# Three fused blocks on one core: engines in source order, weight preparation in equal portions at fixed places, the value product two steps later, VectorE a step behind ScalarE, five weight tiles in flight

## The chip, the core and the metric

The kernel runs on one core of a Trainium2 chip. The core has five engines with queues of their own, each of which runs its queue in order: TensorE (PE in the profile, its weight loads PEld), VectorE (DVE), ScalarE (ACT), GpSimd (POOL) and SyncE (SP), which only issues DMAs. Sixteen DMA engines move data between main memory (HBM) and the on-chip memory SBUF; matmuls write to the eight banks of PSUM. The metric is device time in microseconds.

## The reference

Attention with capped scores on (4 batches, 12 heads, 448 tokens, 64 dims), then two pairs of matmuls (two layers) on 1792 x 768, with inner width 2048. All in float32.

```python
scores = cap * np.tanh(q @ k.T / np.sqrt(64) / cap)
attn = softmax(scores)                        # over the keys
x = (attn @ v)                                # heads side by side: 1792 x 768
h = np.maximum(x @ w_in, 0.0);  y = h * h @ w_out
h = y @ w2_in;  out = h / (1 + exp(-1.702 * h)) @ w2_out
```

## The kernel before

One function, `bounded_cap`, does the whole work (a second one, `any_cap`, is for caps over 40 and is skipped by a branch at the end).

**Attention** goes over 24 pairs of heads. Time is counted in steps T of the source; pair n starts at T = 8n, and `PLAN` (lines 877 to 890) says which function runs how many steps after the start: `load_pair` at -17, key and query transposes and splits (`prep_k`, `prep_q`) from -8 to -3, and for each of four key chunks c the scores product on TensorE (`scores`, L832) at 2c, tanh on ScalarE (L842) at 2c+1, exp on ScalarE (L846) at 2c+2 and the product with v (`pv`, L858) at 2c+3. `take_x` (copies of the two value banks, on ScalarE and VectorE) comes at 10, `divide` (reciprocal on VectorE, multiply on GpSimd, L874, and the store of x) at 11. Within a step the oldest pair comes first. A float32 product in the layers and in the scores is done as three products of a high and a low part (hi x hi, hi x lo, lo x hi); the high part is a rounding copy on ScalarE, the low part a subtraction on VectorE.

**Weight preparation.** The layers multiply 2 x 2 blocks by the seven-product scheme of Strassen and Winograd, so each weight block is turned once into seven matrices that are stored in HBM (`wsa`, `wsb`). One chunk of this is `chunk_steps` (L901): two `load`s of raw weights (64-bit words, of which the wanted bits are joined), two `join`s (L934 on ScalarE, L936 on VectorE), and `sums` (L957 to L960) of four operations, on GpSimd during attention and on VectorE later, with four stores (L947). There are 34 chunks. `weight_group` puts some in a list, `weight_work` pops them in the proportion of the steps gone: 7 chunks over T = 10 to 112, 4 over 130 to 196, then 5 or 6 in each first-product stage (`A_WORK`) and 1 + 2 in a second-product stage (`B_WORK`).

**Layers.** Each of two layers is done in two halves (pairs of batches). In the first-product stage ("a", 56 products of 9 matmuls) a product needs one weight tile of 192 KB, in the second ("b", 21 products of 24 matmuls) two of 256 KB. `load_grain` brings a tile into `wf` (3 buffers) by SyncE's queue, `split_grain` makes the high part (L1047) and the low part (L1048), four tiles ahead of their product (`W_AHEAD`). `split_form` (L1079, L1080) does the same for the moving operands, `x_step` loads and combines those of a half, by SyncE's queue, `b_step` those of the second product from the results of the first. `product` (L1071) issues the matmuls, `after` what reads their banks, `result` the stores, of the last layer alternately by SyncE's and ScalarE's queues.

**What sets the order.** The kernel is written in a language whose scheduler builds each engine's queue: the source gives priorities, and the scheduler moves instructions ahead where it finds their inputs ready in its own model of time. So the place of an instruction in the source is not its place in the queue; the DMA issues of SyncE and GpSimd are moved in the same way. Buffers of a pool are handed out in rotation, and who takes one waits for its last reader.

Of the kernel before, what the change touches and what calls it, by code (L numbers as in the profile page):

```python
# [677 lines left out]
def bounded_cap(ctx, tc, q, k, v, cap, w1, w2, w3, w4, out):  # L678
# [6 lines left out]
    P = 128  # L685
# [18 lines left out]
    w_p = ctx.enter_context(tc.tile_pool(name="w", bufs=6))  # L704
    wf_p = ctx.enter_context(tc.tile_pool(name="wf", bufs=3))
# [7 lines left out]
    e_p = att.enter_context(tc.tile_pool(name="e", bufs=4, side="right"))  # L713
    x_p = att.enter_context(tc.tile_pool(name="x", bufs=3, side="right"))
    ps_m = att.enter_context(tc.tile_pool(name="ps_m", bufs=3, space=PSUM))
    ps_s = att.enter_context(tc.tile_pool(name="ps_s", bufs=2, space=PSUM))
    ps_x = att.enter_context(tc.tile_pool(name="ps_x", bufs=1, space=PSUM))

# [4 lines left out]
    a_ = nc.scalar  # L723

# [146 lines left out]
    def divide(b, p):  # L871
        x, ct = x32.pop((b, p)), pvp.pop((b, p))[2]
        v_.reciprocal(ct, ct)  # L873
        nc.gpsimd.tensor_tensor(x, x, ct, ALU.mult)  # L874
        Q_PUT.dma_start(out=xs[b, p], in_=x)
# [4 lines left out]
        -7: [(prep_k, 1)],  # L880
        -6: [(prep_k, 2), (load_v,)],
        -5: [(prep_q, 0)],
        -4: [(prep_q, 1)],
        -3: [(prep_q, 2)],
# [16 lines left out]
    def chunk_steps(l, kind, i):  # L901
# [25 lines left out]
        def join(u):  # L927
            t = st.pop(("r", u))[:, : 2 * n]

            def words(dt):  # L930
                return t.bitcast(dt).rearrange("p k (f e) -> p k f e", f=P)

            z = sx.bitcast(F16)[:, : 2 * n].rearrange("p k (f t) -> p k f t", t=2)[:, :, :, 1]
            a_.activation(z, words(BF16)[:, :, :, 2], AF.Copy)  # L934
            y = st[u] = y_p.tile([P, 6, P], F32, tag="y", name="wy")
            v_.scalar_tensor_tensor(  # L936
                y[:, : 2 * n].bitcast(I32), words(I32)[:, :, :, 0], 13, sx[:, : 2 * n],
                ALU.logical_shift_right, ALU.bitwise_or,
            )
# [9 lines left out]
        def sums():  # L949
            y1, y2 = st[0], st[1]  # L950
            s = y_p.tile([P, 6, P], F32, tag="y", name="ws")
            t = y_p.tile([P, 3, P], F32, tag="yt", name="wt", bufs=1)
            a11, a12, a21, a22 = (y[:, h * n : h * n + n] for y in (y1, y2) for h in range(2))
            s1, s2 = (s[:, h * n : h * n + n] for h in range(2))
            put(0, y1, 2)
            e = eng[0]
# [10 lines left out]
    eng = [nc.gpsimd]  # L967
# [8 lines left out]
    def weight_group(m):  # L976

        now = [todo.pop(0) for _ in range(m)]
        for n, (load, join, sums) in enumerate(now):
            nxt = now[n + 1][0] if n + 1 < m else lambda u: None  # L980
            if n == 0:
                work.extend([(load, 0), (load, 1)])
            work.extend([(join, 0), (nxt, 0), (join, 1), (sums,), (nxt, 1)])

    def weight_work(k, m):

        if k == 0:
            work_all[0] = len(work)
        while work_all[0] - len(work) < (k + 1) * work_all[0] // m:
            f, *a = work.pop(0)  # L990
            f(*a)

    work_all = [0]
# [44 lines left out]
    def split_grain(n):  # L1038
# [9 lines left out]
        v_.tensor_tensor(y, src, f32(x), ALU.subtract)  # L1048
# [28 lines left out]
    def split_form(key, src, n):  # L1077
        f = forms[key] = f_p.tile([P, 2, NX, S], F32R, tag="f", name="form")
        a_.activation(f[:, 0, :n, :], src, AF.Copy)  # L1079
        v_.tensor_tensor(f[:, 1, :n, :], src, f32(f[:, 0, :n, :]), ALU.subtract)  # L1080

    xin = {}

# [4 lines left out]
    def x_step(l, c, step):  # L1088
# [11 lines left out]
        def sub(o, x, y):  # L1100
            v_.tensor_tensor(xin[o], xin[x], xin[y], ALU.subtract)  # L1101

        if step == 0:
            get("t", left, 0)
            get("u", right, 0)
            form(1, "t")
        elif step == 1:
            get("w", right, NX)
            sub("t", "u", "t")
            form(5, "t")  # L1110
        elif step == 2:
            sub("t", "w", "t")
            form(6, "t")
        elif step == 3:
            sub("u", "w", "u")
            form(7, "u")
            get("u", left, NX)
        elif step == 4:
            form(2, "u")
        elif step == 5:  # L1120
            sub("t", "u", "t")
            form(4, "t")
        else:
            form(3, "w")

    def b_step(l, c, s, ch):
# [4 lines left out]
        def sub(o, x, y):  # L1131
            v_.tensor_tensor(o, x, y, ALU.subtract)  # L1132
# [9 lines left out]
        elif s == 6:  # L1142
            t = gt["t", ch] = wide("tl")[:, :n]
            sub(t, g22, g11)
            form(t)
        elif s == 7:
            sub(g12, g22, g12)
# [25 lines left out]
    def result(l, c, row, col, d, y):  # L1173
# [4 lines left out]
        o = small("t", 2).rearrange("p (c d) -> p c d", d=32)  # L1178
# [57 lines left out]
    if True:  # L1236
        T = -17
        emit_const()
        END = 8 * (len(pairs) - 1) + max(PLAN)
        while T <= END:  # L1240
            attn_sub(T)
            for (t0, t1), m in ATT_WORK:
                if T == t0:
                    weight_group(m)
                if t0 <= T < t1:
                    weight_work(T - t0, t1 - t0)
            if T in X_AT:
                x_step(0, 0, X_AT.index(T))
            if T in G_AT:
                n = G_AT.index(T)  # L1250
                load_grain(n)
                if n:
                    split_grain(n - 1)
            T += 1
        eng[0] = v_
        att.close()
        pool["g"] = ctx.enter_context(tc.tile_pool(name="g", bufs=1, side="right"))
        pool["q"] = ctx.enter_context(tc.tile_pool(name="q", bufs=3, side="right"))
        pool["pa"] = ctx.enter_context(tc.tile_pool(name="pa", bufs=5, space=PSUM))
        pool["pb"] = ctx.enter_context(tc.tile_pool(name="pb", bufs=3, space=PSUM))  # L1260
        loaded, split = len(G_AT), len(G_AT) - 1
        for u, (l, c, kind, s, i) in enumerate(seq):
            if (kind, s, i) == ("a", 1, 0):
                new_g()
                place = {"a": 0, "b": 0}
                if u == 0:
                    hi, lo = wt[0]
                    for n in range(3):
                        b = pool["pb"].tile([P, 512], F32, tag="b", name="pb")
                        nc.tensor.matmul(b[:, :S], hi[:, 0, :], forms[0, 0, "a", 1, 0][:, 0, 0, :], start=True, stop=True)  # L1270
            product(u)
            after(u)
            while split < min(gpos[u] + W_AHEAD + 1, len(grains)):
                if loaded <= split:
                    load_grain(loaded)
                    loaded += 1
                split_grain(split)
                split += 1
                load_grain(loaded)
                loaded += 1  # L1280
            nxt = (l, c + 1) if c == 0 else (l + 1, 0)
            if kind == "a":
                k, order = place["a"], (5, 6, 2)
                if i == NJ - 1 and s in order:
                    b_step(l, c, 1, order.index(s))
                if k == 0:
                    weight_group(A_WORK.get((l, c), 0))
                if k < 7 * NJ - 2:
                    weight_work(k, 7 * NJ - 2)
            else:  # L1290
                k, order = place["b"], (1, 2, 6, 7, 4, 5, 3)
                for (t0, t1), m in B_WORK.get((l, c), ()):
                    if k == t0:
                        weight_group(m)
                    if t0 <= k < t1:
                        weight_work(k - t0, t1 - t0)
                n = order.index(s) + 1
                if n < 7:
                    b_step(l, c, order[n], i)
                if nxt[0] < 2:  # L1300
                    if s == 5 and i == 2:
                        x_step(*nxt, 0)
                    elif s == 3:
                        for st in ((1, 2), (3,), (4, 5, 6))[i]:
                            x_step(*nxt, st)
            place[kind] += 1
# [59 lines left out]
```

## Time and profile before

| | us |
|---|---|
| runs | 1240.38, 1234.47, 1240.67 (median 1240.38) |
| profiled execution, its own time | 1234.58 |
| its span | 1232.7 |
| TensorE busy (matmuls) | 1103.8 (90%) |
| VectorE busy | 845.7 (69%) |
| ScalarE busy | 733.8 (60%) |
| GpSimd busy | 273.8 (22%) |
| mean granted TensorE clock | 0.97 of full speed |

The busy times are sums over the whole span; stages differ much, so the rows below are read by stretches. Matmuls overlap, and a busy TensorE is not one at its peak: the count of matmuls in a stretch says more. In a row of waits the engine and line that waited stand first, then what it waited for.

### The profile page before, as it was taken

To read this page: it belongs to the slowest core of one execution; us is meant where nothing else is said; L and a number is where in the kernel's file an instruction comes from. 1 tells how busy PE (TensorE), PEld (TensorE's weight loads), DVE (VectorE), ACT (ScalarE), POOL (GpSimd) and SP (SyncE) were. 2 spreads that over 40 slices of the span, in tenths; PEclk is the share of its full clock that TensorE was granted. 3 is DMA by queue.
4 is the path that set the end of the run, shared out by engine and by line. 5 is a ranking of instruction groups with operands and counts; after the bars stand their busy time and mean duration, and the time that the engine had idled before them with its cause. 6 is when DMAs were issued, how large, how long until landed. Compare 5 with 4: busy or idle time off the path is not lost.

```text
span 1232.7 us, 15718 instructions
## 1 busy us (share of the span) xinstructions
PE 1103.8 (90%) x5115; PEld 904.7 (73%) x5115; DVE 845.7 (69%) x1089; ACT 733.8 (60%) x1121; POOL 273.8 (22%) x367
## 2 busy tenths in 40 slices
PE   6588988769799999978799999878999998999997
PEld 3244444434489999877679999767999987999996
DVE  3656567858755598585566976677699676559953
ACT  4568777868755666544456655455575536556640
POOL 4657111776510002113310021243000000000000
PEclk9898999989999999998899999989999999999999
DMA  8988434989663338658863576688436464333544
GB/s 213 287 238 261 104 97 118 291 254 299 224 204 108 110 119 275 207 159 299 290 232 114 159 247 192 222 292 259 142 118 189 136 125 131 110 107 123 126 126 73
DMA packets 203757, 227.55 MB, mean 185 GB/s; under 512 B 123794, under 2 KB 160338, under 8 KB 203666
## 3 DMA queue, kind: packets, MB, share of 16 engines
q1 hardware_dynamic: 153234, 118.40, 34.3%
q0 software_dynamic: 28160, 105.30, 25.6%
q10 hardware_dynamic: 22272, 2.76, 1.6%
q8 instruction: 42, 0.69, 0.2%
q14 instruction: 49, 0.40, 0.1%
HBM read 165.84 MB, written 60.56 MB: 184 GB/s over the span
## 4 chain that ended last, share of the span: by engine, by line
PE 46%; DMA 12%; DVE 7%; issue 4%; ACT 3%; POOL 1%; SPq 0%; DVEq 0%; ACTq 0%; POOLq 0%
PE pa L1071 26%; PE pb L1071 20%; DMA wf<-wsa 7%; DMA wf<-wsb 3%; DVE wl L1048 2%; DVE form L1080 2%; ACT form L1079 1%; ACT sx L934 1%; ACT wh L1047 1%; DVE wy L936 1%; DMA wsa<-wy 1%; DVE qu L1201 0%; DVE xl L1101 0%; DMA xl<-ys 0%; DMA wsb<-wy 0%
## 5 line engine op out<-in xcount | busy, mean ns | idle before, releaser
L1071 PE MATMUL pa<-form,wh 128*128 128x448 f32 x1536 | 440.5, 368 | 5.3 <-DVE x L869 2.3
L1047 ACT ACTIVATE wh<-wf 128x384 fp32r<-128x384 f32 (+1 forms) x392 | 219.0, 566 | 306.5 <-DMA wf<-wsa 126.8
L1071 PE MATMUL pb<-form,wh 128*128 128x448 f32 x1152 | 338.5, 376 | 42.0 <-ACT qu L1198 21.7
L1048 DVE TENSOR_TENSOR wl<-wf,wh 128x384 fp32r<-128x384 f32 (+1 forms) x392 | 239.9, 620 | 136.0 <-ACT wh L1047 59.0
L1071 PEld LDWEIGHTS pa<-form,wh 128*128 128x128 f32 x1536 | 290.2, 189 | 32.0 <-DVE x L869 2.7
L1071 PE MATMUL pa<-form,wl 128*128 128x448 f32 x768 | 281.9, 367 | 0.1
L1071 PEld LDWEIGHTS pb<-form,wh 128*128 128x128 f32 x1152 | 219.3, 192 | 70.4 <-ACT qu L1198 28.0
L1071 PE MATMUL pb<-form,wl 128*128 128x448 f32 x576 | 215.4, 374 | 0.7 <-DVE wl L1048 0.7
L858 PE MATMUL vps<-e,v 128*128 128x448 f32 (+1 forms) x384 | 161.9, 594 | 57.1 <-ACT e L846 53.1
L1071 PEld LDWEIGHTS pa<-form,wl 128*128 128x128 f32 x768 | 144.8, 189 | 13.2 <-DVE wl L1048 0.4
L858 PEld LDWEIGHTS vps<-e,v 128*128 128x128 f32 (+1 forms) x384 | 61.4, 198 | 111.9 <-ACT e L846 70.8
L1071 PEld LDWEIGHTS pb<-form,wl 128*128 128x128 f32 x576 | 110.7, 192 | 11.7 <-DVE wl L1048 1.6
L1080 DVE TENSOR_TENSOR form<-g,form 128x1344 fp32r<-128x1344 f32 (+1 forms) x72 | 100.1, 1398 | 18.5 <-ACT form L1079 18.3
L936 DVE SCALAR_TENSOR_TENSOR wy<-wraw,sx 128x768 int32<-128x768 int32 (+1 forms) x68 | 68.0, 1000 | 63.4 <-ACT sx L934 37.3
L832 PE MATMUL sps<-qq,kk 64*128 64x448 f32 (+1 forms) x504 | 103.6, 452 | 5.4 <-ACT e L842 3.0
L934 ACT ACTIVATE sx<-wraw 128x768 f16<-128x768 bf16 (+1 forms) x68 | 69.4, 1020 | 51.9 <-DMA wraw<-in_moe_w_out_dram 20.7
L842 ACT ACTIVATE e<-sps 128x896 f32<-128x896 f32 x96 | 77.6, 812 | 30.6 <-PE sps L832 30.3
L1079 ACT ACTIVATE form<-g 128x1344 fp32r<-128x1344 f32 (+1 forms) x72 | 85.6, 1194 | 10.6 <-DVE g L1132 5.6
L832 PEld LDWEIGHTS sps<-qq,kk 64*128 64x128 f32 (+1 forms) x504 | 55.1, 198 | 49.2 <-issue 24.8
L846 ACT ACTIVATE e<-e,ecap 128x896 f32<-128x896 f32 x96 | 90.2, 944 | 1.8
L873 DVE RECIPROCAL ct<-ct 128x448 f32<-128x448 f32 x24 | 70.8, 2952 | 0.5
L1201 DVE SCALAR_TENSOR_TENSOR g<-pa,qu 128x448 f32<-128x448 f32 x64 | 39.9, 623 | 31.5 <-PE pa L1071 17.2
(76 smaller groups left out, 954.7 us busy)
## 6 DMA issues: line engine op xcount, KB each, us to landing
wf<-wsa SPq DMA_DIRECT2D x224, 192.0 KB, 2.5
wf<-wsb SPq DMA_DIRECT2D x168, 256.0 KB, 2.8
wraw<-in_moe_w_in_dram POOLq DMA_DIRECT2D x32, 766.5 KB, 8.1
wraw<-in_moe_w_out_dram POOLq DMA_DIRECT2D x48, 383.2 KB, 6.4
wsa<-wy POOLq DMA_DIRECT2D x32, 384.0 KB, 6.3
wsb<-wy POOLq DMA_DIRECT2D x24, 384.0 KB, 5.1
wsa<-ws POOLq DMA_DIRECT2D x16, 384.0 KB, 4.8
wraw<-in_moe_w_out_dram POOLq DMA_DIRECT2D x24, 255.5 KB, 5.7
```

The lines of the kernel that those rows point to most:

```text
L832: nc.tensor.matmul(ps[:, u, :S], x, y, start=all(t[0] != u for t in todo[:n]), stop=all(t[0] != u for t in todo[n + 1 :]),)
L842: a_.activation(e, chunk(c, sc.pop((b, p, c)))[:, :, :S], AF.Tanh)
L846: a_.activation(e, e, AF.Exp, scale=ecap)
L858: nc.tensor.matmul(pvp[b, p][j][:, :S], x.rearrange("p a d -> p (a d)"), t, start=c == 0, stop=c == TAIL,)
L873: v_.reciprocal(ct, ct)
L934: a_.activation(z, words(BF16)[:, :, :, 2], AF.Copy)
L936: v_.scalar_tensor_tensor(y[:, : 2 * n].bitcast(I32), words(I32)[:, :, :, 0], 13, sx[:, : 2 * n], ALU.logical_shift_right, ALU.bitwise_or,)
L1047: a_.activation(x, src, AF.Copy)
L1048: v_.tensor_tensor(y, src, f32(x), ALU.subtract)
L1071: nc.tensor.matmul(ps[:, :S], a[:, kk % 4, :], r, start=(s in (1, 5) and kk == 0 and n == 0), stop=(kk == ks - 1 and n == 2), skip_group_c ...
L1079: a_.activation(f[:, 0, :n, :], src, AF.Copy)
L1080: v_.tensor_tensor(f[:, 1, :n, :], src, f32(f[:, 0, :n, :]), ALU.subtract)
```

## The change

It does six things.

- Order: a function `in_order` ties each instruction of `bounded_cap` to the one before it on its engine, SyncE's and GpSimd's DMA issues included, so that each queue has the order of the source.
- VectorE a step behind ScalarE: low parts, shifts of the weight preparation and many subtractions are put in a list `later` and issued by `flush` at the start of the next step or product.
- Weights: the steps of the chunks are popped by `weight_slot`, one `join` or `sums` to a slot, with three loads out ahead. In attention 33 slots for 11 chunks stand 5.5 steps apart from T = 10 on; in the layers three slots per chunk are spread over products 5 to 53 of a first-product stage (6, 6 and 7 chunks) and over products 8 to 13 of the second (2 chunks). The sums always run on VectorE.
- Attention: `pv` at 2c+5, `take_x` at 12, `divide` at 14 with its multiply on VectorE; the preparation of keys and queries is regrouped; the first half's first operand is loaded and split in slices during attention (`x_slice`), its rest in the first products (`x_rest`).
- Loads: `wf` has 5 buffers, the high parts `wh` 5 instead of 6, `e` 5 instead of 4; x loads go to GpSimd's queue.
- Stores: results of the last layer go by GpSimd's queue, and the very last by transposes on TensorE and both other queues. Three warming matmuls come after the first product instead of before it. PSUM pools are declared in another order, so that the layer's first banks are not those of the value product.

```diff
-    w_p = ctx.enter_context(tc.tile_pool(name="w", bufs=6))
-    wf_p = ctx.enter_context(tc.tile_pool(name="wf", bufs=3))
+    w_p = ctx.enter_context(tc.tile_pool(name="w", bufs=5))
+    wf_p = ctx.enter_context(tc.tile_pool(name="wf", bufs=5))
...
+    later = []
+
+    def flush():
+
+        now, later[:] = list(later), []
+        for f in now:
+            f()
...
         v_.reciprocal(ct, ct)
-        nc.gpsimd.tensor_tensor(x, x, ct, ALU.mult)
+        v_.tensor_tensor(x, x, ct, ALU.mult)
...
-        10: [(take_x,)],
-        11: [(divide,)],
+        12: [(take_x,)],
+        14: [(divide,)],
     }
     for c in range(NCH):
-        for i, f in enumerate((scores, tanhs, exps, pv)):
+        for i, f in ((0, scores), (1, tanhs), (2, exps), (5, pv)):
...
+        loads = [(load, u) for load, join, sums in now for u in range(2)]
+        work.extend(loads[:3])
+        del loads[:3]
+        for load, join, sums in now:
+            for u in range(2):
+                work.extend([(join, u), *loads[:1]])
+                del loads[:1]
+            work.append((sums,))
+
+    def weight_slot():
+
+        busy = False
+        while work and (not busy or work[0][0].__name__.startswith("load")):
+            f, *a = work.pop(0)
+            if f.__name__ == "join":
+                f(*a)
+            elif busy or f.__name__ == "sums":
+                later.append(lambda f=f, a=a: f(*a))
+            else:
+                f(*a)
+            busy |= not f.__name__.startswith("load")
...
         a_.activation(x, src, AF.Copy)
-        v_.tensor_tensor(y, src, f32(x), ALU.subtract)
+        later.append(lambda: v_.tensor_tensor(y, src, f32(x), ALU.subtract))
...
-            Q_W.dma_start(out=t, in_=src[b, k0 : k0 + NX].rearrange("k p s -> p k s"))
+            Q_PUT.dma_start(out=t, in_=src[b, k0 : k0 + NX].rearrange("k p s -> p k s"))
...
         for j in range(4):
-            (nc.sync, nc.scalar)[j % 2].dma_start(
+            nc.gpsimd.dma_start(
...
+    def in_order(start):
+
+        last = {}
+        for i in nc.cur_bb.bb.instructions[start:]:
+            if i.engine in last:
+                tc.add_manual_dep(
+                    i, last[i.engine],
+                    mybir.DependencyInfo(mybir.DependencyClass.NoSync, mybir.DependencyReason.DATA),
+                    reason="source order",
+                )
+            last[i.engine] = i.name
...
-ATT_WORK = (((10, 112), 7), ((130, 196), 4))
-X_AT = (114, 116, 118, 120, 122, 124, 126)
+ATT_CHUNKS = 11
+ATT_WORK = tuple(10 + 11 * n // 2 for n in range(33))
+X_AT = tuple(t + 28 * i for i in range(3) for t in (100, 112, 117, 122, 127))
+X_REST = (1, 0, 2, 3, 5)
...
-A_WORK = {(0, 0): 6, (0, 1): 5, (1, 0): 6}
-B_WORK = {(0, 0): (((0, 3), 1), ((9, 16), 2)), (0, 1): (((0, 3), 1), ((9, 16), 2))}
+A_WORK = {(0, 0): 6, (0, 1): 6, (1, 0): 7}
+B_WORK = {(0, 0): ((8, 14), 2), (0, 1): ((8, 14), 2)}
```

## Rows read from the trace of the kernel before

**Rows 1.** Stretches: length, busy time (instructions) per engine, clock, DMA share, GB/s.

```profile
60.00:100.00 40.00, 31.40 (x120) 16.21 (x120) 22.39 (x22) 29.93 (x39) 24.01 (x30) 0.84 0.88 258
100.00:180.00 80.00, 70.19 (x311) 37.36 (x310) 49.31 (x48) 61.34 (x80) 25.73 (x29) 0.99 0.52 142
343.00:440.00 97.00, 94.73 (x467) 87.82 (x468) 54.44 (x92) 57.38 (x111) 3.06 (x5) 1.00 0.43 133
560.00:640.00 80.00, 65.64 (x285) 57.09 (x284) 47.61 (x85) 41.98 (x76) 25.14 (x35) 0.91 0.85 287
```

**Rows 2.** The same view for the join alone (L934): ScalarE busy, clock, DMA.

```profile
343.00:440.00 97.00, 1.08 (x1) 1.00 0.43 133
560.00:640.00 80.00, 11.78 (x11) 0.91 0.85 287
```

**Rows 3.** Waits of the whole run: us in total, times, longest.

```profile
ACT wh L1047 <- DMA wf<-wsa: 126.8, 74, 5.6
...
PE vps L858 <- ACT e L846: 53.1, 37, 6.1
...
ACT sx L934 <- DMA wraw<-in_moe_w_out_dram: 20.7, 8, 4.9
```

**Rows 4.** Timeline at three marks: start, us, engine, line, operation.

```profile
9.89 1.49 PE L832 MATMUL sps<-qq,kk 64*128 64x448 f32 x6 [0.87 <-DVE qq L813]
...
334.65 0.67 PE L1071 MATMUL pa<-form,wh 128*128 128x448 f32 x2 [2.31 <-DVE x L869]
...
1224.35 0.62 DVE L1201 SCALAR_TENSOR_TENSOR qu<-pa,qu 128x448 f32<-128x448 f32 x1 [3.65 <-PE pa L1071]
```

**Rows 5.** The chain that ended last, in order of time: start, us, what.

```profile
354.45 3.65 PE pa L1071 x18
...
543.52 5.65 DMA wf<-wsa
...
596.85 7.56 DMA wf<-wsa
...
643.32 3.72 PE pa L1071 x18
```

**Rows 6.** Groups by line, ScalarE: count, busy us, mean ns, idle before.

```profile
L1047 ACT ACTIVATE wh<-wf 128x384 fp32r<-128x384 f32 (+1 forms) x392 | 219.0, 566 | 306.5 <-DMA wf<-wsa 126.8 <-PE pa L1071 57.3 <-DMA wf<-wsb 55.8
...
L846 ACT ACTIVATE e<-e,ecap 128x896 f32<-128x896 f32 x96 | 90.2, 944 | 1.8
...
L842 ACT ACTIVATE e<-sps 128x896 f32<-128x896 f32 x96 | 77.6, 812 | 30.6 <-PE sps L832 30.3
...
L934 ACT ACTIVATE sx<-wraw 128x768 f16<-128x768 bf16 (+1 forms) x68 | 69.4, 1020 | 51.9 <-DMA wraw<-in_moe_w_out_dram 20.7 <-DVE wy L936 16.1 <-DMA wraw<-in_moe_w_in_dram 13.8
...
L868 ACT ACTIVATE ct<-vps 64x448 f32<-64x448 f32 x48 | 25.8, 538 | 7.3 <-PE vps L858 6.0
```

**Rows 7.** Stretch view for the value banks (vps) alone: PE, PEld, DVE, ACT.

```profile
100.00:180.00 80.00, 43.69 (x110) 16.39 (x111) 8.09 (x14) 7.54 (x14) 0.99 0.52 142
```

**Rows 8.** Groups by line, VectorE and GpSimd.

```profile
L1048 DVE TENSOR_TENSOR wl<-wf,wh 128x384 fp32r<-128x384 f32 (+1 forms) x392 | 239.9, 620 | 136.0 <-ACT wh L1047 59.0 <-PE pb L1071 52.5 <-issue 18.0
...
L922 POOL DMA_DIRECT2D wraw<-in_moe_w_in_dram x32 | 27.2, 851 | 35.1 <-DVE form L1080 12.7 <-DVE wl L1048 9.6 <-DVE g L1132 7.4
...
L957 DVE TENSOR_TENSOR ws<-wy 128x384 f32<-128x384 f32 (+1 forms) x23 | 13.6, 592 | 0.6 <-DMA wsa<-wy 0.2 <-DMA wsb<-wy 0.2
```

**Rows 9.** Timeline from 55 to 60 us, VectorE and GpSimd.

```profile
55.78 4.45 DVE L1048 TENSOR_TENSOR wl<-wf,wh 128x384 fp32r<-128x384 f32 x2
...
56.90 1.00 POOL L958 TENSOR_TENSOR ws<-ws,wy 128x384 f32<-128x384 f32 x1
```

**Rows 10.** DMA issues: count, size of one, median us from issue to landing.

```profile
wraw<-in_moe_w_in_dram POOLq DMA_DIRECT2D x32, 766.5 KB, 8.1
...
out_dram<-qt SPq DMA_DIRECT2D x48, 56.0 KB, 2.7
```

**Rows 11.** Groups by line and shape: the low part of a second-product operand.

```profile
L1080 DVE TENSOR_TENSOR form<-g,form 128x1344 fp32r<-128x1344 f32 x48 | 74.5, 1554 | 17.2 <-ACT form L1079 17.1
```

More of the change, by code (lines that the diff above doesn't have):

```diff
@@ L934, in join, with shift @@
             a_.activation(z, words(BF16)[:, :, :, 2], AF.Copy)
[L935 to L939, printed above, removed]
+            def shift():
+                y = st[u] = y_p.tile([P, 6, P], F32, tag="y", name="wy")
+                v_.scalar_tensor_tensor(
+                    y[:, : 2 * n].bitcast(I32), words(I32)[:, :, :, 0], 13, sx[:, : 2 * n],
+                    ALU.logical_shift_right, ALU.bitwise_or,
+                )
+                if u == 0:
+                    put(0, y, 2)
+            later.append(shift)
         def put(at, t, m):
@@ L978, in weight_group, with weight_slots @@
         now = [todo.pop(0) for _ in range(m)]
[L979 to L989, printed above, removed]
-            f, *a = work.pop(0)
-            f(*a)
-    work_all = [0]
+        loads = [(load, u) for load, join, sums in now for u in range(2)]
[9 more added lines that the diff above has]
+        while work and (not busy or work[0][0].__name__.startswith("load")):
+            f, *a = work.pop(0)
+            if f.__name__ == "join":
[5 more added lines that the diff above has]
+            busy |= not f.__name__.startswith("load")
+    def weight_slots(k, m, n):
+        for _ in range(3 * n * k // m, 3 * n * (k + 1) // m):
+            weight_slot()
     PLACE = {1: 0, 2: 1, 5: 2, 6: 3, 7: 4, 4: 5, 3: 6}
@@ L1234, in new_g @@
             gt[x] = pool["g"].tile([P, NJ, S], F32, tag="g" + x, name="g" + x)
[L1236 to L1278, printed above, removed]
@@ new lines, in in_order @@
+    def in_order(start):
[6 more added lines that the diff above has]
+                    reason="source order",
+                )
+            last[i.engine] = i.name
+    first = len(nc.cur_bb.bb.instructions)
+    T = -17
+    emit_const()
+    END = 8 * (len(pairs) - 1) + max(PLAN)
@@ new lines, in bounded_cap @@
+    while T <= END:
+        flush()
+        attn_sub(T)
+        if T == 2:
+            weight_group(ATT_CHUNKS)
+        if T in ATT_WORK:
+            weight_slot()
+        if T in X_AT:
+            x_slice(*divmod(X_AT.index(T), 5))
+        if T == X_AT[-1] + 1:
+            x_rest(0)
+        if T in G_AT:
+            n = G_AT.index(T)
+            load_grain(n)
+            if n:
+                split_grain(n - 1)
+        T += 1
+    att.close()
+    pool["g"] = ctx.enter_context(tc.tile_pool(name="g", bufs=1, side="right"))
@@ new lines, in bounded_cap @@
+    pool["q"] = ctx.enter_context(tc.tile_pool(name="q", bufs=3, side="right"))
+    pool["pa"] = ctx.enter_context(tc.tile_pool(name="pa", bufs=5, space=PSUM))
+    pool["pb"] = ctx.enter_context(tc.tile_pool(name="pb", bufs=3, space=PSUM))
+    loaded, split = len(G_AT), len(G_AT) - 1
+    for u, (l, c, kind, s, i) in enumerate(seq):
+        if (kind, s, i) == ("a", 1, 0):
+            new_g()
+            place = {"a": 0, "b": 0}
+        flush()
+        product(u)
+        if u == 0:
+            hi, lo = wt[0]
+            for n in range(3):
+                b = pool["pb"].tile([P, 512], F32, tag="b", name="pb")
+                nc.tensor.matmul(
+                    b[:, :S], hi[:, 0, :], forms[0, 0, "a", 1, 0][:, 0, 0, :], start=True, stop=True
+                )
+        while split < min(gpos[u] + W_AHEAD + 1, len(grains)):
+            if loaded <= split:
@@ L1279, in bounded_cap @@
                 load_grain(loaded)
                 loaded += 1
[L1281 to L1305, printed above, removed]
```

153 lines of the change are left out of this document (124 added, 29 removed).

## The prediction

> **What bounds the kernel now.** I read first some stretches of the span side by side [rows 1]. Two things are to be seen. In the first 335 us (attention) no engine is full: from 60 to 100 us TensorE is busy 31.4 of 40 us, at a granted clock of 0.84, while DMA is busy 0.88 of the time; from 100 to 180 us DMA is at 0.52, the clock at 0.99 and TensorE busy 70.2 of 80 us. In the matmul layers TensorE is full where no weight is being prepared (343 to 440 us: 467 matmuls in 97 us, 4.8 per us) and far from it where weights are (560 to 640 us: 285 in 80 us, 3.6 per us, DMA 0.85).
>
> Second, where the weight preparation lies: its `join` on ScalarE ran once in 343 to 440 us and 11 times in 560 to 640 [rows 2]. It comes in bursts, and the poor stretches are the bursts.
>
> Third, the waits [rows 3]. TensorE's value product waits 53.1 us for the exponentials; ScalarE itself stands 20.7 us in `join` for a raw weight, and the exponentials stand behind it in the same queue. In the layers ScalarE's weight split waits 126.8 us for the load of a weight tile (74 waits, the longest 5.6 us).
>
> Fourth, three marks [rows 4]: first scores at 9.89 us, first layer matmul at 334.65, last result read at 1224.35. The span ends at 1232.7 and the run is 1234.58, so 1.9 us lie around the span. The layers thus take 889.7 us. They have 2 layers x 2 halves x (8 x 7 x 9 + 3 x 7 x 24) = 4032 matmuls; 18 of them take 3.65 us in one half and 3.72 in the other [rows 5], so 2016 x 0.2028 + 2016 x 0.2067 = 825.6 us. The other 64 us of the layers are stalls. Attention is 9.89 us of start, 24 pairs of 13.4 us, and about 4 us in which the last pair drains.
>
> **The change, part by part.**
>
> *Attention.* Each engine's order becomes that of the source; the value product goes from step 2c+3 to 2c+5, so that one more scores product stands between an exponential and its use; the weight slots stand 5.5 steps apart; the multiply of x and the weight sums go from GpSimd to VectorE. What is a pair then worth?
>
> ScalarE: tanh 77.6/24 = 3.23, exp 90.2/24 = 3.76, two denominator copies of 0.54, and a key copy of about 0.6 (as a split of that width) [rows 6]: 8.7 us. Eleven chunks have 22 joins: 22 x 1.02/24 = 0.9. The layer's first operand, now cut in slices, is 12 pieces about as long as a split, 12 x 0.57/24 = 0.3. Sum 9.9, and with some 0.05 between 13 instructions 10.6. TensorE: 110 value matmuls from 100 to 180 us [rows 7], 16 a pair, are 6.9 pairs; 70.2/6.9 = 10.2 us busy. VectorE: 49.3/6.9 = 7.2 there, plus the multiply, 0.7 by its width from the 0.59 of a sum [rows 8], plus sums 11 x 4 x 0.59/24 = 1.1 and the shifts, as long as the joins, 0.9: 9.9. So no engine can go below 10.6 a pair.
>
> From above: the quiet stretch as it is, 80/6.9 = 11.6, plus a join for nearly every pair, 12.6. I take 11.2, nearer to the lower end, because what separates 10.6 from 11.6 in that stretch is TensorE waiting for the exponentials, and two steps more are given to them. Attention: 9.9 + 24 x 11.2 + 4 = 283 us (ends 268 and 316), against 334.65.
>
> The sums cost VectorE time but give some back: while GpSimd ran them, two weight subtractions took 4.45 us [rows 9], against 0.62 each on the mean [rows 8]. The reciprocal, VectorE's longest step, now stands two steps behind the copies that free the value banks; nothing of the next pair waits for it.
>
> *Head of line.* `join` stands at a fixed place of ScalarE's queue and waits there for its raw tile; behind it are tanh and exp, and in the layers the reading of finished banks, for which TensorE waits. A raw load lands in 8.1 us [rows 10]. Three loads go out ahead, and each later one when the tile three before it is joined, so it has four slots: 4 x 5.5 steps of 1.4 us = 31 us in attention, 4 x 5 us in the layers. I cost this wait at nothing; that depth is its cover. VectorE's halves run one step later; the low part of a weight is then made a step after the high part, but the split stands four tiles ahead of its product, over 5 us. Cost nothing.
>
> *Layers.* `wf` goes from 3 tiles to 5, and SyncE's queue holds nothing but these loads in the layers (x loads and result stores go to GpSimd's queue), so it runs ahead as far as tiles are free. In the bursts a tile lands in 5.65 to 7.56 us [rows 5]; then come the split, 0.57, and the subtraction, 0.62 [rows 6, 8]. With 3 tiles that is one tile every 2.3 to 2.9 us where TensorE wants one every 9 x 0.2028 = 1.83; the 285 matmuls in 80 us are 2.5 us for every 9, so the depth explains the burst. With 5 tiles, and up to one step (1.8 us) more before the subtraction: (5.65 + 1.2 + 1.8)/5 = 1.7 to (7.56 + 3.0)/5 = 2.1 us. So between no stall and 0.28 us for each first-stage product.
>
> Against this, attention now holds 11 chunks and the layers 23; three first-product stages carry 6, 6 and 7, spread over 49 products (90 us). A chunk is 2 x 766.5 KB in and 7 x 192 KB out, 2.95 MB; 6 in 90 us are 197 GB/s, and TensorE's own tiles 108: up to 305 GB/s, where 287 were carried at 0.85 [rows 1]. The first of these stages had almost no preparation and ran full; it can only lose. I take the middle: 3 x 49 x 0.14 = 21 us, and 1 us at each of four stage starts, where a form is wanted about 1 us before its low part is made: 25. Ends: 0, as in 343 to 440 us, and 64, as now.
>
> In the second-product stages VectorE is the one to watch: three operations of 1.55 us a step [rows 11] and two subtractions of 0.62 are 5.9 us against TensorE's 4.9 for the first three steps, about 4.4 after. Two first-stage products lie between, so the lag stays near 2 us and is picked up. Cost nothing; without that cover 1 to 3 us in each of four stages, inside the ends above.
>
> *Stores and tail.* Result stores go to GpSimd's queue, the very last one through a transpose on TensorE and two queues. Where a store now lands in 2.7 us [rows 10], I leave the end after the last product at 8.3 us, 1 either way.
>
> *Sum:* 283 + 825.6 + 25 + 8.3 + 1.9 = 1144 us, against 1234.58 of the profiled run. That run lies at the low end of the three shown, whose median is 0.5% higher; the sum stands as it is.
>
> **A rule that speaks against it.** A raw load keeps GpSimd 0.85 us in its issue while VectorE is busy 60% of the time [rows 1, 8], so nothing shows that one hinders the other. By the Trainium skill (SBUF — State Buffer, Who interferes with whom), a transfer issued from GpSimd has its descriptors written over a port that some VectorE operations lock, so that it waits, and the page's remedy is SyncE's or ScalarE's queue, the opposite of what is done here; by that the sum would be rival 5's.
>
> **The rivals.**
>
> 1. Depth doesn't cover the landing: 7.56 us and more all the time, first-stage products at 2.1 us, and the layers keep 64 us of stalls: 1144 + 39 = 1183. For it: 305 GB/s wanted. Against: 3 tiles alone explain the burst. 0.17.
> 2. Attention only reaches the quiet stretch plus its joins, 12.6 a pair: 1144 + 34 = 1178. For it: ScalarE and TensorE are within 4% of each other, so little slack smooths their waits. 0.10. Both together, 1217: 0.05.
> 3. It doesn't do what it says: the source's order is as bad as the present one and waits merely change places, 1235: 0.05.
> 4. Slower, by the head of line: if a raw load gets only one slot of lead (5 us of its 8.1), each of 68 joins holds ScalarE 3.1 us, of which TensorE's queued work covers about half: 68 x 1.55 = 105, 1144 + 105 = 1249. It decides from a lead under 8.1 us. For it: in the layers the raw tiles share their three places with x and with temporaries of the second-product stage. Against it, the 20 to 31 us above. 0.08.
> 5. GpSimd's issues are held up: 92 stores in the last stages at 1.5 us instead of 0.85, 4 to a result, make 6 us against the 4.96 of 24 matmuls, about 1 us for each of 23 results: 1167. 0.02.
>
> **How the numbers follow.** The forecast, 1144, has 0.53; its own range is 1110 to 1168 (attention 268 to 300, stalls 5 to 35, not all at once). Range for 8 in 10: from 1110 over rivals 1, 2 and 5 to 1210; it leaves out rivals 3 and 4, the double one and what lies under 1110. Faster by over 0.5%: 0.53 + 0.17 + 0.10 + 0.05 + 0.02 = 0.87; within 0.5%, about what a measurement of this kernel can tell from no change, 0.05; slower 0.08.
>
> **What would show it.** Right: joins evenly spaced over attention, no stretch of it with a clock under 0.95, the value product's wait for exp under 20 us; first layer matmul near 283 us; the split's wait for its loads under half of 126.8 us, and first-product stages with preparation above 4.5 matmuls per us. Wrong: `join` waiting for raw tiles with tanh or exp behind it (rival 4); 2.1 us per 9 matmuls with landings over 7 us (rival 1); over 12 us a pair (rival 2); TensorE waiting for low parts of weights or forms.

## The result: 1114.8 us, and the profile after

The changed kernel takes 1114.78 us (median; 1112.76 to 1119.17) against 1237.43 (1231.57 to 1240.67): 0.902 of the time before, interval 0.897 to 0.907. The forecast was 1144, its range 1110 to 1210. The profiled run took 1114.16 us, its span 1112.4.

The page's first part (busy us, share, instructions) and two rows of its 40 slices, kernel after:

```profile
PE 1069.3 (96%) x5119; PEld 887.4 (80%) x5119; DVE 863.2 (78%) x1173; ACT 722.6 (65%) x1131; POOL 276.6 (25%) x414
...
PE   4999999999999999999999999999999999999997
...
PEclk9999999999999999999999999999999999999999
```

TensorE is busy 90% or more of every slice but the first and the last, and its granted clock is 0.9 or more in all of them. Before, it was 0.84 from 60 to 100 us [rows 1].

Stretches of the kernel after, with the columns of [rows 1]:

```profile
60.00:100.00 40.00, 39.21 (x181) 21.00 (x180) 33.91 (x41) 36.49 (x49) 10.79 (x16) 1.00 0.89 241
60.00:220.00 160.00, 154.40 (x718) 83.88 (x718) 142.34 (x172) 148.75 (x199) 50.41 (x76) 1.00 0.90 241
...
300.00:340.00 40.00, 40.00 (x199) 37.06 (x198) 28.28 (x53) 25.64 (x49) 14.86 (x21) 1.00 0.82 276
540.00:580.00 40.00, 40.00 (x199) 37.08 (x198) 33.22 (x53) 30.25 (x53) 9.09 (x13) 1.00 0.79 269
700.00:740.00 40.00, 40.00 (x199) 37.08 (x198) 32.37 (x60) 26.36 (x52) 17.01 (x24) 1.00 0.94 309
```

From 60 to 100 us TensorE went from 120 to 181 matmuls [rows 1], under the same DMA share. The last three stretches lie in the three first-product stages that now carry weight preparation: 199 matmuls in 40 us, 5.0 per us, where a burst before ran 3.6 [rows 1].

The join alone in two stretches of attention (ScalarE busy, clock, DMA share, GB/s), to be read against [rows 2]:

```profile
100.00:140.00 40.00, 4.10 (x5) 1.00 0.89 234
...
180.00:220.00 40.00, 4.25 (x4) 1.00 0.89 239
```

Four or five in each 40 us, and the clock at 1.00: even portions, as planned. They are also fewer. The join over the whole of attention, in the kernel before and in the kernel after:

```profile
0.00:334.60 334.60, 34.56 (x34) 0.94 0.75 215
...
0.00:260.30 260.30, 22.84 (x22) 1.00 0.82 221
```

The source of before lays 22 joins into attention as well; its scheduler had pulled twelve more ahead, as many as the source has in the first stage of the layers, of which almost none were left there (one in 343 to 440 us, [rows 2]). Attention thus also got shorter by work that the layers now carry.

Waits of the whole run (us in total, times, longest), to be read against [rows 3]:

```profile
ACT wh L1070 <- DMA wf<-wsa: 27.1, 17, 4.8
...
DVE wl L1071 <- ACT wh L1070: 22.8, 20, 2.4
...
ACT wh L1070 <- DMA wf<-wsb: 20.4, 5, 6.7
...
PE pa L1094 <- DVE form L1103: 5.8, 5, 2.0
...
PE pa L1094 <- DVE wl L1071: 5.3, 6, 1.5
```

The split's wait for the first kind of weight tile fell from 126.8 to 27.1 us. The value product's wait for the exponentials, 53.1 us before, has no row left. What the layers' matmuls still wait for most is low parts, of operands and of weights: 5.8 and 5.3 us.

Two groups by line (busy, mean ns, idle before), kernel after:

```profile
L942 ACT ACTIVATE sx<-wraw 128x768 f16<-128x768 bf16 (+1 forms) x68 | 69.4, 1021 | 0.9 <-DVE wy L946 0.9
L1276 POOL DMA_DIRECT2D out_dram<-o x92 | 57.9, 636 | 253.9 <-DVE o L1274 250.6 <-issue 1.9 <-DMA xl<-ys 1.4
```

The join waits for no raw load in the whole run (before, 20.7 and 13.8 us for the two kinds of raw load, [rows 6]), and a store keeps GpSimd 0.64 us.

Two marks of the timeline (start, us, engine, line):

```profile
260.31 0.68 PE L1094 MATMUL pa<-form,wh 128*128 128x448 f32 x2
...
1103.54 0.62 DVE L1296 SCALAR_TENSOR_TENSOR qu<-pa,qu 128x448 f32<-128x448 f32 x1 [3.08 <-PE pa L1094]
```

The first layer matmul is at 260.31 us instead of 334.65, the last result is read at 1103.54 instead of 1224.35 [rows 4]. So of the 120.3 us between the two spans attention gave 74.3 and the layers 46.5 (889.7 to 843.2); the tail lost 0.5 (8.35 to 8.86).

### The profile page after: what moved, and what is told of

It is laid out like the page before. It is cut to its first block, busy times and chain, and to the rows that moved or that the text cites. A ratio compares the mean times of both kernels' runs of the same rounds, so it can differ in the third digit from the quotient of the medians.

```text
span 1112.4 us, 15612 instructions
## 1 busy us (share of the span) xinstructions
PE 1069.3 (96%) x5119; PEld 887.4 (80%) x5119; DVE 863.2 (78%) x1173; ACT 722.6 (65%) x1131; POOL 276.6 (25%) x414
## 4 chain that ended last, share of the span: by engine, by line
PE 59%; DVE 14%; issue 8%; DMA 5%; ACT 4%; POOL 1%; DVEq 0%; ACTq 0%; POOLq 0%
PE pb L1094 28%; PE pa L1094 27%; DVE form L1103 3%; DMA wf<-wsa 3%; DVE wl L1071 3%; PE vps L867 2%; PE sps L841 1%; DMA out_dram<-o 1%; DVE ct L882 1%; ACT sx L942 1%; DVE g L1215 1%; DVE g L1296 1%; DVE qu L1296 1%; ACT e L851 1%; ACT e L855 1%
## 5 line engine op out<-in xcount | busy, mean ns | idle before, releaser
L1094 PE MATMUL pb<-form,wh 128*128 128x448 f32 x1152 | 329.4, 367 | 2.0 <-DVE form L1103 1.1
L1070 ACT ACTIVATE wh<-wf 128x384 fp32r<-128x384 f32 (+1 forms) x392 | 211.3, 560 | 66.2 <-DMA wf<-wsa 27.1
L1071 DVE TENSOR_TENSOR wl<-wf,wh 128x384 fp32r<-128x384 f32 (+1 forms) x392 | 225.4, 607 | 27.7 <-ACT wh L1070 22.8
L1094 PE MATMUL pb<-form,wl 128*128 128x448 f32 x576 | 210.8, 366 | 0.0
L867 PE MATMUL vps<-e,v 128*128 128x448 f32 (+1 forms) x384 | 148.1, 552 | 2.3 <-DVE x L878 2.2
L1276 POOL DMA_DIRECT2D out_dram<-o x92 | 57.9, 636 | 253.9 <-DVE o L1274 250.6
L841 PE MATMUL sps<-qq,kk 64*128 64x448 f32 (+1 forms) x504 | 92.6, 419 | 0.9 <-DVE qq L822 0.9
L1293 ACT ACTIVATE qu<-pb 128x448 f32<-128x448 f32 x88 | 47.5, 540 | 68.7 <-PE pb L1094 65.1
L946 DVE SCALAR_TENSOR_TENSOR wy<-wraw,sx 128x768 int32<-128x768 int32 (+1 forms) x68 | 61.7, 908 | 37.3 <-ACT sx L942 37.3
L841 PEld LDWEIGHTS sps<-qq,kk 64*128 64x128 f32 (+1 forms) x504 | 50.0, 190 | 46.6 <-ACT kk L810 13.0
```

What stands on the lines that cost most here:

```text
L841: nc.tensor.matmul(ps[:, u, :S], x, y, start=all(t[0] != u for t in todo[:n]), stop=all(t[0] != u for t in todo[n + 1 :]),)
L867: nc.tensor.matmul(pvp[b, p][j][:, :S], x.rearrange("p a d -> p (a d)"), t, start=c == 0, stop=c == TAIL,)
L946: v_.scalar_tensor_tensor(y[:, : 2 * n].bitcast(I32), words(I32)[:, :, :, 0], 13, sx[:, : 2 * n], ALU.logical_shift_right, ALU.bitwise_or,)
L1070: a_.activation(x, src, AF.Copy)
L1071: later.append(lambda: v_.tensor_tensor(y, src, f32(x), ALU.subtract))
L1094: nc.tensor.matmul(ps[:, :S], a[:, kk % 4, :], r, start=(s in (1, 5) and kk == 0 and n == 0), stop=(kk == ks - 1 and n == 2), skip_group_c ...
```

## The experiments

The first four below ran beside the kernel before at 1228.47 us, the next four beside it at 1237.09, the last four beside it at 1236.99. Differences under 0.5% are not read from a single time. "Attention" is the time of the first layer matmul (260.3 us in the kernel after, 334.65 before), "the layers" what follows up to the start of the last one (842.8 after, 889.2 before).

**free_order: the order by source left out.**

```diff
-    in_order(first)
```

> The changed kernel without the tie of each engine to source order; every buffer count, place and queue of the change stays. Theory A (the order is the cause: equal portions stand only where the queue keeps them): the scheduler pulls weight preparation ahead again, joins come in bursts, and most of the gain goes: 1190 to 1240 us, first layer matmul after 310 us. Theory B (the buffers, the later value product and the deeper loads are the cause, the order only an aid): within 2% of the changed kernel, 1115 to 1140 us.

1164.99 us: attention 310.5, the layers 843 as they were. The time lies between the two bands, but A's signs are there: the order alone is worth 50 us, all of it in attention. The join in two stretches and over all of attention, columns as above:

```profile
60.00:100.00 40.00, 7.49 (x7) 0.96 1.06 322
100.00:140.00 40.00, 6.43 (x6) 0.93 1.11 310
...
0.00:310.50 310.50, 34.61 (x34) 0.93 0.83 240
```

With the scheduler free the joins bunch, 7 and 6 in 40 us, with the DMA share over 1 and the clock at 0.93 to 0.96; and 34 of them run in attention instead of 22. The layers are no shorter for having twelve fewer. So the order does two things: it keeps the portions even, and it leaves twelve joins with their loads and sums to the layers, which take the same 843 us with them. Which of the two makes how much of the 50 us was not tried; 22 joins in bunches cost 9 us (bursts, below).

**before_ordered: the kernel before, with its order fixed by source and nothing else.**

```diff
+    first = len(nc.cur_bb.bb.instructions)
     if True:
...
+    in_order(first)
```

> The kernel before with its engines tied to source order and nothing else. Theory A in its plain form (the order alone does it): well under 1200 us. Theory C (source order pays only where the source is laid out for it: value product two steps later, VectorE a step behind, three loads out ahead): slower than before, over 1250 us, with ScalarE waiting in join for raw weights and VectorE waiting for ScalarE.

1457.23 us, 229 more than the kernel before beside it. Attention gains some 14 us (321.0), but the layers take about 1125 instead of 889. Two of its waits:

```profile
DVE wl L1048 <- ACT wh L1047: 309.2, 164, 6.2
...
PE pa L1071 <- ACT wh L1047: 65.1, 35, 9.7
```

VectorE stands 309 us for the split (59.0 before, [rows 8]), as theory C had it, and TensorE's matmuls wait for it, which they never do in the kernel after; ScalarE's waits in the join, the other sign of C, stay at 7 us. So the order by source is no gain in itself; it pays for a source laid out for it, with loads far enough ahead.

**depth3: the weight tiles back to three.**

```diff
-    wf_p = ctx.enter_context(tc.tile_pool(name="wf", bufs=5))
+    wf_p = ctx.enter_context(tc.tile_pool(name="wf", bufs=3))
```

> The changed kernel with 3 weight-load tiles instead of 5. The prediction's step (5.65 to 7.56 us of landing plus 3.0 over 3 tiles is 2.9 to 3.5 us a tile where one is wanted every 1.83): the three first-product stages with preparation lose 49 products x about 1 us each, 1115 + 100 to 150 where landing stays that long, at least 1115 + 40. Rival (spacing alone made loads land early enough): 1115 to 1125, wait of the split for its loads still about 50 us.

1188.06 us: attention unchanged (259), the layers 918, 75 more, between the expected 40 and 100 to 150. Its waits:

```profile
ACT wh L1070 <- DMA wf<-wsb: 136.9, 65, 7.3
ACT wh L1070 <- DMA wf<-wsa: 128.2, 79, 5.3
```

The 27.1 and 20.4 us of the kernel after become 128.2 and 136.9. Without the depth the new layers would be slower than the old ones (918 against 889). By the starts of the matmuls 45 of the 75 us lie in the three first-product stages with preparation and 28 in the second-product stages, which the formula of the prediction did not cover.

**before_depth5: the kernel before with five weight tiles** (and five instead of six of the split ones).

```diff
-    w_p = ctx.enter_context(tc.tile_pool(name="w", bufs=6))
-    wf_p = ctx.enter_context(tc.tile_pool(name="wf", bufs=3))
+    w_p = ctx.enter_context(tc.tile_pool(name="w", bufs=5))
+    wf_p = ctx.enter_context(tc.tile_pool(name="wf", bufs=5))
```

> The kernel before with 5 weight-load tiles instead of 3 (and 5 high-part tiles instead of 6, for room), order left to the scheduler. If depth alone makes the layers' gain: layers 889 us down to 843 to 855, attention unchanged at about 330, total 1185 to 1200. If spacing or SyncE's free queue is needed as well: layers over 870, total over 1210.

1200.33 us, 37 less than before beside it; attention unchanged (334.6), the layers 855. The burst of [rows 1]:

```profile
560.00:640.00 80.00, 73.84 (x344) 66.67 (x344) 51.82 (x94) 46.73 (x89) 22.72 (x32) 0.96 0.82 279
```

344 matmuls where there were 285, at the same DMA share (0.82 against 0.85). The stretch holds 9 joins against 11; the whole stage holds 12 in both, and takes 115 us instead of 134. So memory was not full in the burst; too few loads were under way. Depth alone gives 35 of the 46.5 us of the layers; by the starts of the matmuls 28 of these are stalls and 6 to 7 come from the spacing of the matmuls (last section), which nothing here ties to the depth.

**pv_early: the value product back at step 2c+3.**

```diff
-        for i, f in ((0, scores), (1, tanhs), (2, exps), (5, pv)):
+        for i, f in ((0, scores), (1, tanhs), (2, exps), (3, pv)):
```

> The changed kernel with the value product back at 2c+3. If its two steps took away the wait for exp: attention about 1 to 1.5 us a pair longer, 24 to 36 us, total 1140 to 1150, with a wait of the value product for exp of over 25 us. If source order alone took it away: 1115 to 1120.

1169.58 us, attention 313.5: 53 us longer, where 24 to 36 were expected, and for another reason:

```profile
PE vps L867 <- DVE x L878: 34.1, 23, 2.3
...
PE vps L867 <- ACT e L855: 9.8, 23, 1.2
```

TensorE waits for the value banks, not for the exponentials: the next pair's first product now stands at step 11, ahead of the step (12) at which VectorE empties them. That run couldn't tell what the two steps are worth, hence the next.

**pv_early2: the same, with the banks emptied two steps sooner too.**

```diff
-        12: [(take_x,)],
-        14: [(divide,)],
+        10: [(take_x,)],
+        12: [(divide,)],
...
+        for i, f in ((0, scores), (1, tanhs), (2, exps), (3, pv)):
```

> The changed kernel with the value product at 2c+3 and, unlike the run before, the copies of the value banks and the division two steps earlier too (10 and 12), as in the kernel before, so that the next pair's first value product does not stand ahead of them. If those 53 us were the banks: first layer matmul near 265 us, total about 1120. If the two steps for exp are worth something by themselves: 275 to 300 us, with the value product's wait for exp over 15 us.

1158.94 us, attention 303.9, just above the second band. Its two longest waits between TensorE and ScalarE in attention:

```profile
ACT e L851 <- PE sps L841: 55.3, 62, 4.4
...
PE vps L867 <- ACT e L855: 38.0, 23, 2.5
```

Now it is the exponentials, and both engines wait for each other in turn, since scores stand behind the waiting value product. Two steps more between an exponential and its use are worth up to 44 us.

**bursts: the weight slots 2.75 steps apart instead of 5.5.**

```diff
-ATT_WORK = tuple(10 + 11 * n // 2 for n in range(33))
+ATT_WORK = tuple(10 + 11 * n // 4 for n in range(33))
```

> The changed kernel with its 33 attention slots 2.75 steps apart instead of 5.5, so all eleven chunks lie in the first half of attention. If equal portions matter: pairs of the first half go over 11.5 us (a join every 3.5 us, DMA at its limit, raw loads late), second half under 9.9; first layer matmul 10 to 30 us later than 260. If only the total counts: within 5 us of 260.

1125.37 us, attention 269.1, between the two bands. Stretches as in [rows 1]:

```profile
60.00:100.00 40.00, 33.79 (x137) 18.35 (x135) 35.55 (x42) 31.12 (x40) 15.40 (x22) 0.87 1.10 326
...
140.00:220.00 80.00, 79.44 (x372) 43.18 (x370) 68.91 (x81) 73.69 (x102) 14.41 (x24) 1.00 0.62 167
```

The loaded first stretch loses more (137 matmuls against 181, clock 0.87) than the relieved one wins (372 against 355 in the kernel after). Equal portions are worth about 9 us, the least of the three attention edits. The three taken back singly cost 50, 44 and 9 us, 103 together, where all of attention's gain is 74: they don't add.

**no_lag: VectorE's halves issued at once, not a step behind ScalarE.**

```diff
+    class Now(list):
+
+        def append(self, f):
+            f()
+
+    later = Now()
```

> The changed kernel with everything in the list issued at once, so VectorE is no step behind ScalarE and deferred loads go out at once. If the step matters (in order, VectorE stands for each high part and the copies behind it are late): VectorE's waits for ScalarE up by over 50 us, attention and layer stage starts longer, 1125 to 1160. If the queues have slack enough: within 5 us of 1115.

1109.25 us, a little under the second band; attention 259.4, the layers 838.8. VectorE's wait for the split doubles (22.8 us in the kernel after), and nothing is late by it:

```profile
DVE wl L1076 <- ACT wh L1075: 47.5, 56, 2.4
```

The step behind ScalarE, part of the change, is worth nothing here; a single time doesn't show whether it costs the 4 us by which the layers are shorter.

**pool_sums: the multiply of x and the sums back on GpSimd, in attention.**

```diff
-        v_.tensor_tensor(x, x, ct, ALU.mult)
+        nc.gpsimd.tensor_tensor(x, x, ct, ALU.mult)
...
-            e = v_
+            e = eng[0]
```

> The changed kernel with the weight sums of attention and the multiply of x back on GpSimd. VectorE has 11 x 4 x 0.53 + 24 x 0.63 = 38 us less to do in attention. If it was near setting the pair (37 of 40 us busy): attention shorter, 250 to 258 us. If two engines on one pair of operands hinder each other (4.45 us for two subtractions in the trace of before): VectorE's mean for a subtraction goes up again and attention is 5 to 20 us longer. If VectorE has slack and the sums run beside it: 258 to 263.

1117.22 us, attention 259.8: no difference. From 60 to 220 us:

```profile
60.00:220.00 160.00, 154.75 (x721) 84.31 (x720) 122.28 (x125) 148.69 (x200) 102.82 (x123) 1.00 0.89 238
```

VectorE is 20 us less busy than in the kernel after and GpSimd 52 more, and TensorE does the same 154 us. This move, too, is worth nothing. That a subtraction beside a sum on GpSimd takes longer [rows 9] is seen here again (`xt<-xw,xt` takes 1.62 us on the mean of two, 0.62 in the kernel after), and it costs attention nothing.

**no_join: ScalarE's half of the join left out in attention** (22 of 68 joins; what it would write is missing from those weights).

```diff
-            a_.activation(z, words(BF16)[:, :, :, 2], AF.Copy)
+            if not attn[0]:
+                a_.activation(z, words(BF16)[:, :, :, 2], AF.Copy)
```

> The changed kernel without the join's half on ScalarE during attention (22 of its 68 are left out, so the weights prepared there are wrong). If ScalarE sets the 9.9 us of a pair, about 22 x 1.0 us go: first layer matmul near 240 us. If TensorE sets it: 257 to 260 as now.

**less_pe: the third part of the scores product left out** (low part of the key by high part of the query).

```diff
-            todo = [(0, kk[:, ik, cols], qq[:, iq, :]) for ik, iq in ((0, 0), (0, 1), (1, 0))]
+            todo = [(0, kk[:, ik, cols], qq[:, iq, :]) for ik, iq in ((0, 0), (0, 1))]
...
```

> The changed kernel without the third part of each scores product (low key x high query left out, so scores are less exact): TensorE has some 1.0 us less per pair. If TensorE sets the pair: about 24 us go, first layer matmul near 238 us. If ScalarE does: 257 to 260. If both move it by half, they set it in turns.

no_join: 1113.91 us, attention 256.2. less_pe: 1108.19 us, attention 252.8. Both lie outside their bands, between the two theories. The stretch from 60 to 220 us, first of no_join:

```profile
60.00:220.00 160.00, 157.52 (x741) 86.27 (x740) 143.94 (x175) 138.97 (x188) 52.40 (x79) 1.00 0.93 248
```

and of less_pe:

```profile
60.00:220.00 160.00, 147.76 (x624) 75.04 (x622) 146.62 (x178) 152.25 (x204) 51.78 (x78) 0.99 0.94 250
```

With ScalarE relieved of 22 us TensorE is at 98% and 4 us are won. With a third of the scores gone, 7 of a pair's 45 matmuls, ScalarE is at 95% and 7.5 us are won. Neither engine alone sets the pair: with TensorE at 96.5, ScalarE at 93 and VectorE at 89%, whichever is relieved, the next is there at once.

**best: no_lag, the later operand slices made in the order of their use, and x loaded four places sooner in one stage.**

```diff
-                x_step(l, c, k + 5)
+                x_step(l, c, (6, 5, 7)[k])
...
-        if kind == "b" and nxt[0] < 2 and place["b"] == 14:
+        if kind == "b" and nxt[0] < 2 and place["b"] == (10 if (l, c) == (1, 0) else 14):
```

> The changed kernel without the step between ScalarE and VectorE, with form 2 of a first-product stage made before form 3 (it is wanted at product 3, form 3 at product 9), and with the last half's x loads issued four products earlier. If the stalls that are left in the layers are operands made just too late at stage starts: about 1.4 us less in each of three stages and 2 to 4 us less where the x loads stood behind result stores, 1100 to 1106 against 1109. If they come from VectorE's total load there, no change: 1107 to 1111.

1106.08 us (1101.23 to 1107.88), 0.893 of the kernel before, interval 0.887 to 0.898, where the kernel after has 0.897 to 0.907: likely 0.8% faster than that, though the ends of the intervals still overlap. The layers take 837.9 against 838.8 in no_lag, so by the times nearly all of the gain is that of no_lag. TensorE's waits for the low part of an operand in the layers, first of no_lag, then of best, tell more:

```profile
PE pa L1099 <- DVE form L1108: 6.2, 7, 1.4
...
PE pa L1099 <- DVE form L1108: 3.7, 5, 1.1
```

Two waits of 1.4 us, at the stage starts near 475 and 681 us, are gone: the order of the slices does mend these. The layers' time hides it, since in best more matmuls run at the slower of two spacings (last section), 2.1 us in all. The wait for a high part at the start of the last half is 2.0 us in no_lag and 2.1 in best, so the x loads issued sooner mend nothing there.

Not tried singly: x loads and result stores on GpSimd's queue, the operand slices in attention, the preparation spread over the layers' stages, the order of the PSUM pools and the place of the warming matmuls.

## Where the prediction was right, and where it was off

*Direction, range and the marks.* Of what it named as signs all appeared but one: even joins, clock 1.00, no wait for exp, the split's wait at a fifth, first-product stages at 5.0 matmuls per us. The first layer matmul came at 260.31 us, not near 283. The time, 1114.16 against 1144, is 30 us lower, near the low end. By terms, forecast and measured:

| term | forecast | measured | difference |
|---|---|---|---|
| start of attention | 9.9 | 10.0 | +0.1 |
| 24 pairs | 24 x 11.2 = 268.8 | 24 x 10.08 = 241.9 | -26.9 |
| what is left of attention (fill, drain) | 4 | 8.4 | +4.4 |
| matmuls of the layers | 825.6 | 821 | -4.6 |
| stalls of the layers (the rest of their time) | 25 | 22.2 | -2.8 |
| tail, and what lies around the span | 10.2 | 10.6 | +0.4 |

*The step that failed: "So no engine can go below 10.6 a pair."* The value banks alone in the kernel after (TensorE, its loads, VectorE, ScalarE):

```profile
60.00:220.00 160.00, 96.55 (x254) 39.07 (x254) 19.86 (x32) 17.26 (x32) 1.00 0.90 241
```

254 value matmuls, 16 a pair, are 15.9 pairs in 160 us: 10.08 us a pair, under the floor. The floor was ScalarE's sum of durations, 9.9, with 0.05 us between 13 instructions. Its queue in the kernel after, a stretch of the timeline:

```profile
53.77 1.04 ACT L855 ACTIVATE e<-e,ecap 128x896 f32<-128x896 f32 x1
54.71 0.90 ACT L851 ACTIVATE e<-sps 128x896 f32<-128x896 f32 x1
55.65 1.04 ACT L855 ACTIVATE e<-e,ecap 128x896 f32<-128x896 f32 x1
```

The exponential lasts 1.04 us, but the instruction behind it starts 0.94 us after it. Four of these in a pair are up to 0.4 us that a sum of durations counts twice, and the gaps that I added are there only behind the tanh (0.04). Added up one by one, ScalarE's instructions from 60 to 220 us come to 158 us, 10.0 a pair, as forecast; its busy time, which counts an overlap once, is 148.75/15.9 = 9.4 us a pair; TensorE's is 154.4/15.9 = 9.7, not the 10.2 read from the quiet stretch [rows 1, 7]. So the bound was about 9.7, and the kernel runs within 4% of it. The second half of the mistake is the 11.2 itself, put between a floor that was too high and the old stretch: the wait for exp did not shrink but vanished.

*Layers: nearly the right sum, by luck, for a wrong place.* I gave 21 us to the first-product stages and 1 us to each of four stage starts. Stretches of 20 us in the kernel after (TensorE busy, clock, DMA share, GB/s); a full one has 98.6 starts of matmuls at 0.2028 us, and shows one or two more, since a matmul that reaches over an edge is counted on both sides:

```profile
260.00:280.00 20.00, 17.38 (x80) 1.00 0.67 221
460.00:480.00 20.00, 17.94 (x87) 1.00 0.63 195
680.00:700.00 20.00, 17.94 (x88) 1.00 0.75 243
780.00:800.00 20.00, 18.21 (x86) 1.00 0.38 125
800.00:820.00 20.00, 19.03 (x94) 1.00 0.46 138
880.00:900.00 20.00, 16.69 (x77) 1.00 0.55 156
900.00:920.00 20.00, 20.00 (x91) 0.91 0.30 92
```

The stages with preparation are full (199 in 40 us, in the result above). The stage starts are short: read from the starts of the matmuls in the trace, they lose 4.6, 2.6, 2.6, 3.6 and 6.5 us, 19.9 in all, the first of them the layers' own start; of the last, 1.3 lie just before the stage's start at 890.8 us. TensorE waits there mostly for the low parts of operands and weights (5.8 and 5.3 us in the waits above, a few of these elsewhere), which was the last of the signs that the prediction gave for being wrong; the latest of them also has the clock at 0.91.

*The formula of the five tiles* was fed with 5.65 to 7.56 us, pieces of the chain that ended last [rows 5], which are long landings and not the usual ones. From issue to landing in the burst of before (560 to 640 us), and in the first-product stage of the first layer's second half in depth3 (480 to 602 us):

```profile
DMA to landing us min/median/max: 2.3/5.2/7.6
...
DMA to landing us min/median/max: 2.3/3.6/7.2
```

The chain of the kernel after even has longer ones than 7.56, while its median is 3.9 us (issues: count, KB, median us to landing):

```profile
wf<-wsa SPq DMA_DIRECT2D x224, 192.0 KB, 3.9
```

The chain that ended last, in the kernel after:

```profile
396.51 43.78 PE pb L1094 x216
...
543.54 9.27 DMA wf<-wsa
...
815.43 39.62 PE pb L1094 x192
...
1029.11 44.64 PE pb L1094 x216
```

With 3.9 in the formula five tiles give (3.9 + 3.0)/5 = 1.4 us a tile, with 5.2 they give 1.6, both under the 1.83 that TensorE wants, so no stall; and a single landing of 9.27 us is borne by the tiles ahead of it (199 matmuls from 540 to 580 us). For three tiles it gives (3.6 + 3.0)/3 = 2.2 us, and the 56 products of that stage of depth3 took 122 us, 2.2 each.

*Matmul rate.* I gave half of the matmuls 0.2067 us, as before [rows 5]. After, most take 0.2028 (43.78/216) and about 800, in the last two second-product stages, 0.2067 or near it (39.62/192 and 44.64/216): 4032 x 0.2028 + 800 x 0.0039 = 821, 5 us less.

*The rivals.* None came. Depth covers the landing (1; 309 GB/s were carried from 700 to 740 us with TensorE full, and depth3 shows that it is the depth). A pair takes 10.1, not 12.6 (2). Source order is as bad as feared in before_ordered, but not here (3). The join waits for no raw load (4). A store on GpSimd takes 0.64 us, less than the 0.85 of a raw load before [rows 8], with VectorE busy 78% of the time (5). The rule of the Trainium skill behind this rival (SBUF — State Buffer, Who interferes with whom) is for VectorE's copies, casts and `tensor_scalar` in a two-port mode; the page says that `tensor_tensor` has no such mode. From 807 to 1102 us, where the stores stand, VectorE ran no copy and no `tensor_scalar`, so these rows don't test the rule.

*Edits costed right:* moving sums and multiply to VectorE, and its step behind ScalarE, at nothing. The tail, 8.9 us, lies within its bound of 8.3, 1 either way.

## What to carry to other kernels

An order fixed by source and places fixed by hand are one edit: the same order cost 229 us on a source not laid out for it, and the same places lost 50 us without it. Give loads depth by their rate (median landing plus the steps behind it, over the tiles) before moving work around them: 35 of 46.5 us of the layers came with two more tiles. For a floor, take an engine's busy time over a well-filled stretch, not a sum of single durations plus gaps; where three engines are within 8% of each other, no cut on one of them brings what it takes away.

## What the runs showed of the hardware that I had not expected

An instruction on ScalarE behind an exponential of 1.04 us started 0.94 us after it, behind a tanh of 0.90 us 0.94 after it (rows above).

The layer matmuls go at one of two spacings at a granted clock of 1.00, 0.2028 or 0.2067 us, constant over a long run of them (216 in 43.78 or 44.64 us). Which stage has which differs between kernels that do the same work there: the same 216 of the first second-product stage take 43.78 us in the kernel after and 44.64 in free_order, both with TensorE full and the clock at 1.00. All 4032 at one or the other is 16 us. What sets it was not tried and stays open; the 5 us above are thus explained in size, not in cause.
